# The first x tile loaded in two column halves, and the first value product moved up between two transposes

## The chip, the cores and the metric

The kernel runs on one core of one Trainium2 chip. The metric is the device time of one execution in microseconds (us), lower is better. The time before is 286.43 us, the median of three runs that lie between 286.04 and 286.88 us.

## The reference

The reference mixes two branches over the same x of 2048 tokens by 640 columns, in bfloat16, with a gate per token. Branch a is a linear attention with 32 heads of 20 columns and softmax feature maps; branch b is a SwiGLU block with 1728 hidden columns.

```python
x = A_x                                             # 1 x 2048 x 640
g = _sigmoid((x * gate_w).sum(-1, keepdims=True))
qkv = x @ wqkv                                      # q, k, v of 32 heads
...
kv = jnp.einsum("bhsf,bhsd->bhfd", phi_k, v)
...
a = o @ wo
b = (silu(x @ w_gate) * (x @ w_up)) @ w_down
return g * a + (1 - g) * b
```

## The kernel before, in words

**Tiling.** The 2048 tokens are 16 tiles of 128 tokens. For most products the kernel needs x transposed, with the 640 columns as 5 chunks of 128 on the partitions: the buffer `xT` holds chunk c of tile t as `xT[:, t, c, :]`. Tiles 0 to 3 are loaded as they are into `xs` and transposed by TensorE (PE) against an identity, with a copy from PSUM to `xT` behind it; tiles 4 to 15 are transposed by the DMA. The value weights are in `wvg`, five chunks of 128 rows with 640 columns, and one more column (640) that the kernel fills with `gate_w`, so that one product gives the values and the gate's sum.

**Order.** Nothing reorders the program. Two strings list it: `LOADS` gives the order in which the loads are issued, and `ORDER` that of the work. A small recorder (`run`, line 145) adds the waits on semaphores that the buffers' readers and writers need. Each engine goes through its own instructions in that order, so an instruction that waits holds back all that stands behind it on its engine. One call of `mm` (line 302) or `transposes` (line 319) is one unit for the recorder: all that any of its matmuls reads must be there before its first one starts.

**Queues.** Loads are issued by SP and by ACT, each through a DMA queue of its own. `XQ` and `WQ` (lines 376 and 377) give the issuer of each x tile and each value weight chunk. SP issues x tile 0, gate_w (`g`), w1, w2, w3 and then the first columns of the gate and up weights (`f0`); ACT issues w0, x1, x2, x3, w4 and, behind these, loads its activation table and does its copies.

**The work around the change.** `H0` to `H12` are 26 matmuls on a constant that feed nothing. `X0.0` transposes chunk 0 of tile 0 (its copy is on DVE), `X0.1` chunks 1 to 4 (its copy is on ACT); `X1` and `X2` do both parts of tiles 1 and 2 with both copies on DVE, `X3` does tile 3 in one part. `G` turns gate_w into a column with one small matmul, and DVE casts it into column 640 of `wvg`. `Ut.c` (`vpart`, line 525) adds chunk c of the value product of tile t: two matmuls of 320 and 321 columns, one for each half of the columns, into the two PSUM banks of a pair. Only the second half reads column 640. `U0.0` is thus the first product with real data; it needs `xT` chunk 0 of tile 0 and w0, and as one unit also the column from `G`. `h` is a step that ACT alone runs: it waits for w3 and issues two small loads. From `F0.1` on the feed-forward products follow, whose weights are `f0`.

PSUM is used as four pairs of banks; `next_pair` (line 475) gives the one that was used longest ago. `U1.0` writes the pair that `X0` used, so it also waits until both copies of `X0` have read it.

Of the kernel before, what the change touches and what calls it, by code (L numbers as in the profile page):

```python
# [6 lines left out]
P = 128  # L7
S_TOK = 2048
D = 640
# [21 lines left out]


LOADS = """
x0 w0 x1 g w1 x2 w2 x3 w3 w4 f0 k0 k1 t4 k2 k3 k4 k5 t5 t6 t7 t8 t9 t10 t11 t12 t13 t14 t15 q0 q1 q2 q3 q4 q5
 f1 f2
"""

ORDER = """
H0 H1 H2 H3 H4 H5 H6 H7 H8 H9 H10 H11 H12 X0.0 G X0.1 X1 h U0.0 U1.0 U0.1 X2 U1.1 U2.0 U0.2 U1.2 U2.1 X3 U2.2
U0.3 U1.3 U2.3 U0.4 U1.4 U2.4 V3 Y i4 F0.1 M0 M1 F0.2 M2 V4 M3 M4 F0.0 M5 K0 i3 K1 S0 I P0 K3 S1 P1  # L40
F1.0 K2 V6 E0 V8 K4 S2 S3 E1 S4 K5 S5 P2 P3 V7 E2 V5 R0 K6 P4 P5 R2 E3 K7 S6 E4 V15 K8 E5 V10 S7 P6
K9 E6 R1 P7 S8 K10 S9 E7 K11 S10 V9 V11 P8 E8 K12 P9 R3 E9 P10 K13 S11 E10 K14 S12 P11 V12 S13 E11
# [11 lines left out]
class _Tracker:  # L54
# [90 lines left out]
    def run(self, eng, fn, reads=(), writes=(), dma=False):  # L145
        rkeys = list(dict.fromkeys(k for a in reads for k in self.keys_of(a)))
        wkeys = list(dict.fromkeys(k for a in writes for k in self.keys_of(a)))
        need = {}

        def req(ev, raw):  # L150
            if ev is None:
                return
            s, v = ev
            if s == eng and not dma and (eng == "pe" or not raw):
                return
            if v > need.get(s, 0):
                need[s] = v

        for k in rkeys:
            for kk in self._conflicts(k):  # L160
                req(self.lastw[kk], True)
                if k[0] == "psum":
                    for s, v in self.readers[kk].items():
                        req((s, v), False)
        for k in wkeys:
            for kk in self._conflicts(k):
                req(self.lastw[kk], True)
                for s, v in self.readers[kk].items():
                    req((s, v), False)
        self._wait(eng, need)  # L170
        ins = fn()
        if dma:
            sn = "d%d" % self.ndma
            self.ndma += 1
            self._add_sem(sn)
            inc = 16
        else:
            sn, inc = eng, 1
        ins.then_inc(self.sem[sn], inc)
        self.cnt[sn] += inc  # L180
        v = self.cnt[sn]
        snap = dict(self.known[eng])
        if not dma:
            snap[sn] = max(snap.get(sn, 0), v)
        self.evknow.setdefault(sn, {})[v] = snap
        ev = (sn, v)
        for k in wkeys:
            self.lastw[k] = ev
            self.readers[k] = {}
        for k in rkeys:  # L190
            r = self.readers[k]
            if r.get(sn, 0) < v:
                r[sn] = v
        return ev


def _build(nc, A_x, A_wqkv, A_w_phi, A_wo, B_x, B_w_gate, B_w_up, B_w_down, gate_w, out):
    tr = _Tracker(nc)
    pe, act, dve, pool, sp = nc.tensor, nc.scalar, nc.vector, nc.gpsimd, nc.sync
# [68 lines left out]
    def at(name, shape, dtype, rel):  # L268
        n = mybir.dt.size(dtype)
        for s in shape[1:]:  # L270
            n *= s
        assert rel + n <= SLAB, (name, rel + n, SLAB)
        t = nc.alloc_sbuf_tensor_at(name, list(shape), dtype, offset=sbase + rel)
        tr.reg(t, "sbuf", sbase + rel)
        return t
# [4 lines left out]
    xs = at("xs", [P, NPE, D], BF16, 10752)  # L280
# [10 lines left out]
    def bank(b, c0, c1, r0=0, r1=P):  # L291
        return ps[r0:r1, b * 512 + c0:b * 512 + c1]
# [9 lines left out]
    def mm(pairs):  # L302
        reads, writes = [], []
        for p in pairs:
            reads += [p[1], p[2]]
            writes.append(p[0])

        def fn():
            last = None
            for o, l, r, st, sp_, sk in pairs:  # L310
                last = pe.matmul(o, lhsT=l, rhs=r, start=st, stop=sp_, skip_group_check=sk)  # L311
            return last
        return run("pe", fn, list({id(a): a for a in reads}.values()), writes)
# [45 lines left out]
    def dma(e, dst, src, transpose=False):  # L359
        eo = tr.eng[e]  # L360

        def fn():
            if transpose:
                return eo.dma_start_transpose(dst, src)
            return eo.dma_start(dst, src)  # L365
        rd = [src] if src.tensor.name in tr.base else []
        wr = [dst] if dst.tensor.name in tr.base else []
        return run(e, fn, rd, wr, dma=True)
# [7 lines left out]
    XQ = ["sp", "act", "act", "act"]  # L376
    WQ = ["act", "sp", "sp", "sp", "act"]
    x2 = A_x[0]
# [3 lines left out]
        return dma(e, dst, A_wqkv[c * P:(c + 1) * P, c0:c0 + D])  # L382

    def load_x(t):
        dma(XQ[t], xs[:, t, :], x2[t * P:(t + 1) * P, :])

    def load_xt(t):
        dma("sp", xT[:, t, :, :], x2[t * P:(t + 1) * P, :], transpose=True)
# [81 lines left out]
    def used(r):  # L470
        ring["lru"].remove(r)
        ring["lru"].append(r)
        return r

    def next_pair():
        return used([r for r in ring["lru"] if r < ring["n"] and r not in held][0])
# [31 lines left out]
    def v_pairs(t, pr):  # L508
        return [(bank(2 * pr + hb, 0, 320 + hb), xT[:, t, c, :], wvg[:, c, 320 * hb:640 + hb - 320 * (1 - hb)],
                 c == 0, c == 4, False) for c in range(5) for hb in range(2)]  # L510

    def v_out(t, pr):
        i = halves(pr).rearrange("p b (h d) -> p b h d", d=DH)
        o = vbuf(t)[:, 0:H * (DH + 1)].rearrange("p (b h d) -> p b h d", b=2, d=DH + 1)[:, :, :, 0:DH]
        copy("act", o, i)
        copy("act", svec[:, t:t + 1], bank(2 * pr + 1, 320, 321))
# [6 lines left out]
    vpr = {}  # L523

    def vpart(t, c):

        if c == 0:
            vpr[t] = next_pair()
            held.add(vpr[t])
        mm(v_pairs(t, vpr[t])[2 * c:2 * c + 2])  # L530
        if c == 4:
            held.remove(used(vpr[t]))
            v_out(t, vpr[t])
# [302 lines left out]
    def kv_end():  # L836
# [4 lines left out]

    ops = {
        "H": lambda i: warm(), "i": fills, "X": xpose, "G": gcol, "U": vpart, "V": vtile,
        "M": lambda m: premult(1, m), "R": lambda m: premult(0, m),
        "K": ktile, "S": knorm, "P": kmul, "p": lambda t: kmul(t, "dve"), "E": kvtile, "x": load_x, "t": load_xt, "w": load_wv, "g": load_gate, "h": load_phi, "k": lambda m: load_wt(1, m), "q": lambda m: load_wt(0, m),
        "f": lambda i: load_ffn(FCUT[i], FCUT[i + 1]), "L": load_late_weights, "T": tail_weights, "J": gates,
        "Y": w_blocks, "I": kv_begin, "N": kv_end, "Z": z_row,
# [50 lines left out]
```

## Time and profile before

| what | value |
|---|---|
| median of three runs | 286.43 us (286.04 to 286.88) |
| the profiled execution's own time | 286.45 us |
| its span from the first to the last instruction | 285.2 us |
| PE busy | 282.2 us, 99% of the span, 1999 matmuls |
| DVE, ACT, POOL busy | 61%, 52%, 55% |
| from 6.63 to 7.30 us: PE busy | 0.46 of 0.67 us |
| from 7.30 to 11.55 us: PE busy | 4.25 of 4.25 us |

The profile is one execution seen by the hardware profiler; times within it count from the span's start. A busy PE need not be doing useful work at its full rate: the 26 constant matmuls count as busy, and a matmul's time on the page (about 0.22 to 0.48 us in the first microseconds) is its latency, while the distance from one start to the next is what it costs when many follow each other. The chain of waits that the page prints goes back from the last instruction to what released each one; what stands on it sets the end.

### The profile page before, as it was taken

Reading aid. Unit: us, or ns where it says so; the run is one execution under the profiler, and the core shown is the slowest. Engines: PE = TensorE matmul, PEld = TensorE weight load, DVE = VectorE, ACT = ScalarE, POOL = GpSimd, SP = SyncE. Lnnn points to the kernel's source line nnn. Section 1 sums busy time; section 2 is a strip of 40 time slices with the busy share of each in tenths; the row PEclk is TensorE's granted clock in tenths of the full one; section 3 lists DMA queues with packets and bytes.
Section 4 is the critical chain, followed back from the end, with each engine's and each line's share of the span. In section 5 each row is a group of like instructions: output and inputs, shape, how many; then the busy total and the mean of one; then the engine's idle time right before and its main releaser. Section 6 shows DMA issues by size and latency. Waiting matters only on the chain.

```text
span 285.2 us, 5063 instructions
## 1 busy us (share of the span) xinstructions
PE 282.2 (99%) x1999; PEld 174.6 (61%) x1999; DVE 174.3 (61%) x265; ACT 148.1 (52%) x258; POOL 155.9 (55%) x120
## 2 busy tenths in 40 slices
PE   8999999999999999999999999999999999999997
PEld 6656777766645444545544547767767545767766
DVE  2246667784689975998799756898962627200000
ACT  2577787786755655666566676224323457321122
POOL 6186988987157759869688643473540563100000
PEclk9999999999999999999999999999999999999999
DMA  7975779100010952522031200166243030010011
GB/s 208 242 119 127 118 139 373 68 3 0 3 47 0 275 154 57 105 54 51 0 71 33 52 0 7 37 96 143 55 113 85 3 74 1 11 47 25 23 46 48
DMA packets 50727, 22.20 MB, mean 78 GB/s; under 512 B 40815, under 2 KB 50567, under 8 KB 50703
## 3 DMA queue, kind: packets, MB, share of 16 engines
q1 hardware_dynamic: 49174, 21.00, 31.7%
q10 hardware_dynamic: 1529, 0.87, 1.1%
q8 instruction: 16, 0.26, 0.4%
q14 instruction: 8, 0.07, 0.1%
HBM read 9.38 MB, written 2.62 MB: 42 GB/s over the span
## 4 chain that ended last, share of the span: by engine, by line
PE 97%; DMA 2%; SPq 0%; DVE 0%; issue 0%
PE ps L311 97%; DMA wvg<-in_A_wqkv_dram 2%; SPq L365 0%; PE ps L323 0%; DVE osb L824 0%
## 5 line engine op out<-in xcount | busy, mean ns | idle before, releaser
L311 PE MATMUL ps<-xT,wg 128*128 128x512 bf16 x260 | 64.6, 379 | 0.0
L311 PE MATMUL ps<-xT,wu 128*128 128x512 bf16 x260 | 64.6, 379 | 0.0
L339 POOL TENSOR_TENSOR hT<-hT,us 128x512 bf16<-128x512 bf16 (+1 forms) x36 | 42.1, 1175 | 33.5 <-DVE hT L343 21.6
L339 POOL TENSOR_TENSOR ph<-eq,qc 128x1320 bf16<-128x1320 bf16 x16 | 40.4, 2524 | 31.7 <-DVE qc L659 16.9
L311 PE MATMUL ps<-wqk,xT 128*128 128x320 bf16 x320 | 47.9, 299 | 0.0
L329 ACT ACTIVATE us<-ps 128x512 bf16<-128x512 f32 (+1 forms) x60 | 34.1, 568 | 20.5 <-PE ps L311 19.8
L311 PEld LDWEIGHTS ps<-xT,wu 128*128 128x128 bf16 x260 | 25.4, 98 | 30.7
L311 PEld LDWEIGHTS ps<-xT,wg 128*128 128x128 bf16 x260 | 25.1, 98 | 28.2 <-ACT oT L329 0.6
L339 POOL TENSOR_TENSOR ekr<-ekr,krec 128x1280 bf16<-128x1280 bf16 x16 | 37.3, 2358 | 5.8 <-DVE krec L353 5.8
L343 DVE SCALAR_TENSOR_TENSOR hT<-hT,ps 128x512 bf16<-128x512 bf16 (+1 forms) x39 | 24.9, 641 | 25.2 <-ACT hT L329 20.9
L311 PE MATMUL ps<-wd,hT 128*128 128x320 bf16 (+3 forms) x295 | 40.2, 296 | 0.0
L329 ACT ACTIVATE osb<-ps,omg 128x640 bf16<-128x640 f32 (+2 forms) x17 | 12.4, 755 | 52.9 <-PE ps L311 52.9
L311 PEld LDWEIGHTS ps<-wqk,xT 128*128 128x128 bf16 x320 | 30.5, 98 | 12.6
L311 PEld LDWEIGHTS ps<-wd,hT 128*128 128x128 bf16 (+1 forms) x295 | 26.9, 98 | 11.1 <-issue 1.3
L329 ACT ACTIVATE eq<-ps 128x640 bf16<-128x640 f32 x32 | 22.3, 703 | 19.1 <-PE ps L311 11.9
L339 POOL TENSOR_TENSOR hx<-hx,us 128x512 bf16<-128x512 bf16 (+1 forms) x20 | 24.1, 1213 | 11.5 <-DVE hx L343 5.9
L350 DVE TENSOR_REDUCE ksum<-ekr 128x64 f32<-128x1280 bf16 x16 | 23.4, 1464 | 11.0 <-ACT ekr L329 11.0
L329 ACT ACTIVATE hT<-ps 128x512 bf16<-128x512 f32 (+1 forms) x39 | 22.0, 563 | 13.4 <-PE ps L311 11.2
L329 ACT ACTIVATE ekr<-ps 128x640 bf16<-128x640 f32 x32 | 22.3, 703 | 6.9 <-PE ps L311 6.4
L311 PE MATMUL ps<-wvg,xT 128*128 128x320 bf16 (+1 forms) x160 | 24.6, 302 | 0.2 <-DMA wvg<-in_A_wqkv_dram 0.2
L311 PE MATMUL ps<-wog,oT 128*128 128x320 bf16 (+2 forms) x165 | 24.7, 295 | 0.0
L350 DVE TENSOR_REDUCE qz<-eq 128x64 f32<-128x1280 bf16 x16 | 23.4, 1480 | 1.7 <-ACT eq L329 1.7
(86 smaller groups left out, 283.7 us busy)
## 6 DMA issues: line engine op xcount, KB each, us to landing
out_dram<-osb SPq DMA_DIRECT2D x15, 160.0 KB, 1.8
wd<-in_B_w_down_dram SPq DMA_DIRECT2D x1, 2080.0 KB, 8.7
wg<-in_B_w_gate_dram SPq DMA_DIRECT2D x1, 1040.0 KB, 8.7
wu<-in_B_w_up_dram SPq DMA_DIRECT2D x1, 1040.0 KB, 10.8
wog<-in_A_wo_dram SPq DMA_DIRECT2D x2, 375.0 KB, 4.2
wg<-in_B_w_gate_dram SPq DMA_DIRECT2D x1, 640.0 KB, 5.2
wu<-in_B_w_up_dram SPq DMA_DIRECT2D x1, 640.0 KB, 6.4
xs<-in_A_x_dram ACTq DMA_DIRECT2D x3, 160.0 KB, 4.2
```

The costliest lines, as they stand in the source:

```text
L311: last = pe.matmul(o, lhsT=l, rhs=r, start=st, stop=sp_, skip_group_check=sk)
L329: return run("act", lambda: act.activation(o, i, func, scale=scale), rd, [o])
L339: return run(e, lambda: eo.tensor_tensor(o, a, b, op), [a, b], [o])
L343: return run("dve", lambda: dve.scalar_tensor_tensor(out=o, in0=a, scalar=s, in1=b, op0=op0, op1=op1), rd, [o])
L350: return run("dve", lambda: dve.tensor_reduce(o, i, AX.X, ALU.add), [i], [o])
```

## The change

Two things change, both in the first microseconds.

The load of x tile 0 becomes two: columns 0 to 383 (chunks 0 to 2, 96 KB) on SP's queue, and columns 384 to 639 (chunks 3 and 4, 64 KB) on ACT's queue. Both are the first issue of their queue, so ACT's five other loads, its table load and its copies each stand one issue further back.

In the order of the work, `X0.1` comes ahead of `G`, and `U0.0` comes between `G` and `X1`. `U0.0` is now two units for the recorder, one for each half of the columns, so that the first half doesn't wait for the gate's column. The instructions are otherwise the same, and none is added on PE, DVE or POOL. In `LOADS`, `g` and `x1` change places, but they are on different queues.

As the pairs of banks are given out in order of use, `U0` and `X1` exchange theirs (pairs 0 and 2), and with them all later users of these two; the order of reuse stays.

```diff
 LOADS = """
-x0 w0 x1 g w1 x2 w2 x3 w3 w4 f0 k0 k1 t4 ...
+x0 w0 g x1 w1 x2 w2 x3 w3 w4 f0 k0 k1 t4 ...
...
 ORDER = """
-H0 ... H12 X0.0 G X0.1 X1 h U0.0 U1.0 U0.1 X2 U1.1 U2.0 U0.2 U1.2 U2.1 X3 U2.2
+H0 ... H12 X0.0 X0.1 G U0.0 X1 h U1.0 U0.1 X2 U1.1 U2.0 U0.2 U1.2 U2.1 X3 U2.2
...
     def load_x(t):
-        dma(XQ[t], xs[:, t, :], x2[t * P:(t + 1) * P, :])
+        if t == 0:
+            for e, c0, c1 in (("sp", 0, 384), ("act", 384, D)):
+                dma(e, xs[:, t, c0:c1], x2[t * P:(t + 1) * P, c0:c1])
+        else:
+            dma(XQ[t], xs[:, t, :], x2[t * P:(t + 1) * P, :])
...
-        mm(v_pairs(t, vpr[t])[2 * c:2 * c + 2])
+        vp = v_pairs(t, vpr[t])[2 * c:2 * c + 2]
+        for m in ([vp[0:1], vp[1:2]] if t == c == 0 else [vp]):
+            mm(m)
```

## The prediction, made before the changed kernel ran

> **What bounds the kernel now.** I read the chain of waits first, cut to its first 12 us. Its columns are start, length, what.
>
> ```profile
> 1.66 0.36 SPq L365
> 2.02 0.04 issue
> 2.06 5.20 DMA wvg<-in_A_wqkv_dram
> 7.26 0.05 issue
> 7.30 0.99 PE ps L311 x6
> ```
>
> One transfer sets the start: the value weight chunk w2, issued by SP at 2.06 and landed at 7.26. At 7.30 PE begins U0.2, and from there the chain is PE to the end (97% on the page). So the change is worth what it moves U0.2's start, and nothing before 7.30 that PE can absorb in waiting. The order of time shows what PE did until then (start, length, then the work; in brackets the idle time before it and what ended it).
>
> ```profile
> 0.84 2.93 PE L504 MATMUL ps<-const-bfloat16-1.0 128*128 128x128 bf16 x26 [0.84 <-PEq L883]
> 1.26 1.42 ACTq L365 DMA_DIRECT2D xs<-in_A_x_dram  x3
> 3.19 1.28 ACT L329 ACT_TABLE_LOAD   x1 [3.19 <-issue]
> 3.69 0.10 PEld L323 LDWEIGHTS ps<-ident,xs 128*128 128x128 bf16 x1 [0.18 <-DMA xs<-in_A_x_dram]
> 3.95 0.10 PEld L311 LDWEIGHTS ps<-ident,gwr 128*128 128x128 bf16 x1 [0.16 <-DMA gwr<-in_gate_w_dram]
> 4.00 1.12 PE L323 MATMUL ps<-ident,xs 128*128 128x128 bf16 x9
> 4.63 0.60 ACT L329 ACTIVATE xT<-ps 128x512 bf16<-128x512 bf16 x1 [0.16 <-PE ps L323]
> 5.80 0.12 PEld L311 LDWEIGHTS ps<-wvg,xT 128*128 128x128 bf16 x2 [0.20 <-DMA wvg<-in_A_wqkv_dram]
> 6.10 0.44 PE L323 MATMUL ps<-ident,xs 128*128 128x128 bf16 x5
> 7.30 0.66 PEld L311 LDWEIGHTS ps<-wvg,xT 128*128 128x128 bf16 x6 [0.55 <-DMA wvg<-in_A_wqkv_dram]
> 8.41 3.43 PE L311 MATMUL ps<-wvg,xT 128*128 128x320 bf16 x24
> ```
>
> PE waits for x0 (0.18), for gate_w (0.16), for w1 (5.80) and for w2 (0.55 on the weight side; the last matmul before it starts at 6.78 and costs 0.136, so PE itself stood for 0.38). Two paces show. A transpose costs (1.12 - 0.31) / 8 = 0.10 us around 4 and (0.44 - 0.22) / 4 = 0.055 us at 6.1; a 320-column matmul costs 0.27 us at 4.92 (two take 0.74 with a last one of 0.475) and (3.43 - 0.30) / 23 = 0.136 from 8.41. PE's pace doubles between 5.45 and 5.8.
>
> Issue times plus the time to landing give the loads: x0 0.80 + 2.8 = 3.6, w0 0.80 + 3.0 = 3.8, x1 1.26 + 3.0 = 4.3, w1 1.66 + 4.1 = 5.8, x2 1.73 + 4.2 = 5.9, w2 2.06 + 5.2 = 7.3, x3 2.22 + 5.2 = 7.4, w3 2.53 + 5.6 = 8.1, w4 2.70 + 5.6 = 8.3, the gate weights 3.00 + 6.8 = 9.8, the up weights 3.48 + 7.7 = 11.2.
>
> **The change, step by step.**
>
> *x0.* Half the queue work lies in each queue, so both parts should land ahead of 3.6. The constant matmuls hold PE until 3.46 + 0.11 = 3.57, which is as early as X0.0 can be: 0.12 earlier than 3.69. If the halves land no earlier than 3.6, this is 0.
>
> *X0.1 ahead of G.* Four transposes at 0.107 follow at once, 3.67 to 4.10, and G at 4.10 finds gate_w landed (3.9). G's wait of 0.16 is covered by transposes.
>
> *U0.0.* Its first half needs DVE's copy of X0.0, which ended 0.56 after X0.0's start (3.69 to 4.25), so 4.13, and w0. w0 is now ACT's second issue: between 3.8 (where it was) and 4.3 (x1, second now, behind 160 KB instead of 64); I take 4.1, nearer the middle as it has 64 KB ahead. So it runs 4.15 to 4.42. The second half needs the gate's cast, which ended 0.40 after G's start (3.96 to 4.36): 4.50. It runs 4.52 to 4.79; 0.10 idle.
>
> *X1.* Queued behind U0.0 on PE, it goes from 4.38 to 4.79 and ends at 5.32. x1 lands between 4.3 and 4.8 (one more issue of 0.45 ahead), and is covered. DVE's copy of X1.0 ended 0.58 after X1's start: 5.37 now.
>
> *ACT's extra issue.* Three issues take 1.42, so one is 0.45 or so, and the table load goes from 3.19 to 3.64 and ends at 4.92 instead of 4.47. X0.1's copy, which waited 0.16 for PE, now waits for the table: 4.92 to 5.52 instead of 4.63 to 5.23. U1.0 writes X0's banks and waits for it; its load came 0.11 behind that copy (5.34), so 5.61 now. This loses 0.27 of what came before. Queued behind U1.0 on PE are U0.1 and all else. ACT has no other work until 8.17, where it waits for w3.
>
> *From U1.0 to U2.0.* At the fast pace: U1.0 5.61 to 5.9; U0.1 (w1 at 5.8 is there) to 6.17; X2 at 6.2, since x2 lands between 5.9 and 6.4 (one issue later; I take 6.1), to 6.48; U1.1 to 6.75; U2.0 0.63 after X2's first load, as before (6.00 to 6.63): 6.83 to 7.10. It ended at 6.92 before. So PE is ready for U0.2 at 7.10, and the most that this order can gain is 7.30 - 7.10 = 0.20 us. Were ACT's copy not late, U2.0 would end at about 6.9 and the most would be 0.4.
>
> *w2.* SP's queue has 64 KB less ahead of it, ACT's 64 KB more. From 5.0 to 8.2 the two moved 313 GB/s, so 64 KB are 0.21 us at the whole rate and 0.42 at half. Against that, w1 and w2 are issued no earlier, and from 4.2 to 5.2, where w1 and w2 were moving, the rate was only 213 GB/s, with x0 long done: then the gain is 0. I take 0.15, below the middle, as x0's bytes were through by 3.6 and w2 moved later. U0.2 would start at 7.15.
>
> *Queue arbitration.* The Trainium skill (DMA: Bandwidth & Descriptors, Queues, rings and completion order) says that each DMA engine goes round robin between the queues that have work. By that rule ACT's 64 KB more wouldn't hold w2 back, and w2 would gain the 0.42 of half the rate; the sum would then be PE's 0.20, not w2's 0.15. No row of before separates the two.
>
> *Behind U0.2.* 0.15 earlier, X3 needs x3 at 7.85 (7.4, at most 0.45 later: 7.85, just covered), U0.3 needs w3 at 8.4 (8.1), U0.4 w4 at 9.2 (8.3 to 8.8), the first feed-forward product the gate weights at 11.4 (9.8), the up weights at 12.4 (11.2). All are covered. Further on PE has no idle time that could take the gain back.
>
> *Sum:* 7.15 - 7.30 = -0.15 us. The profiled execution took 286.45 (span 285.2 and 1.25 around it), the median is 286.43: 286.3 either way.
>
> **The rivals.**
>
> *w2 does not move:* the change does what it says before 7 us, and PE waits longer for the same landing. For it: w2 is issued at the same time and moved in the slow stretch. Against it: less lies ahead. 286.4; up to 286.8 if ACT's extra bytes do cost it 0.42.
>
> *Everything lands early:* w1, x2 and w2 all come before PE is ready. PE then runs U1.0 at 5.61 and, without the wait for x2, ends U2.0 at about 7.03: 0.27 gained, 286.15. A gain above 0.4 has no mechanism here, as PE's own work and ACT's copy fill the time.
>
> *The pace doubles later (slower):* in before the pace doubled at about 5.6, after PE had been nearly without holes since 0.84. Now a hole of 0.29 (5.32 to 5.61) and one of 0.10 (4.42 to 4.52) lie right ahead of that place; in return the holes of 0.12 and 0.16 near 3.7 go. If the doubling comes later, U1.0, U0.1, U1.1 and U2.0 cost 8 x 0.13 more and X2 5 x 0.05 more: 1.3, of which 0.2 is hidden by the wait for w2: +1.1, 287.5; lasting through U0.2 to X3, seven more matmuls or so, up to 2.1. It decides if the transposes of X2 still follow each other at 0.107. The profile's granted clock is 1.00 in all stages, so only the spacing shows it. The Trainium skill (TensorE: Matmul & The Clock Gate, Part 1) puts this doubling at the end of a free-running window of about 3.4 us in which PE was busy. By that rule the moment varies from run to run; the doubling 4.7 us after PE's first matmul agrees, and what hole counts as idle no run here shows.
>
> *w0 holds X1 back:* U1.0 would follow w0's landing by 1.2 (U0.0 0.53, X1.0 and its copy 0.58, two releases). That matters only from w0 at 4.6 on; x1's row bounds it at 4.3. Every 0.1 beyond costs 0.1.
>
> **How the numbers follow.** The forecast (0 to 0.2 gained) gets 0.57, w2 unmoved 0.18, all early 0.10, the later doubling 0.13, w0 0.02. Runs of the same kernel spread from 286.04 to 286.88, so I call 0.3% (0.86 us) the limit of what can be told from no change. No case of gain reaches it by itself; with that scatter 0.07 of the forecast and 0.05 of the early case end beyond it: faster 0.12. Slower: 0.11 of the doubling, and 0.05 from scatter of the others, 0.16. The rest is 0.72. The forecast's own range, with the scatter of the median, is 285.9 to 286.7. The range 285.8 to 287.2 takes in the unmoved and early cases and the beginning of the slow one, and leaves out about 0.09 above and 0.06 below.
>
> **What would show it.** Right: X0.0 at about 3.57, G with no wait behind X0.1, U0.0 from about 4.15, ACT's table load at about 3.64 and U1.0 released by ACT's copy at about 5.6, U0.2 at 7.1 to 7.2, PE unbroken behind it. Wrong: U0.2 earlier than 7.0 (ACT's copy did not hold U1.0), at 7.3 or later with w2 its releaser (w2 unmoved), transposes at 0.107 in X2 (pace), or a new wait for x3 or w4 behind 7.3.

## The result: slower, 288.24 us against 286.15

The changed kernel takes 288.24 us (median of 19 runs, 286.72 to 290.12), the kernel before 286.15 (19 runs, 285.83 to 287.79). The ratio of the means is 1.0063, with a 95% interval from 1.005 to 1.0077. The forecast was 286.3, its range ended at 287.2.

The 19 times are not one cloud: nine lie from 286.72 to 287.58 (mean 287.2), ten from 288.24 to 290.12 (mean 289.0), and none between. So there are two costs to find: one of about 0.8 us in every execution (the lower group's mean against 286.35, the mean of before) and one of about 1.9 us in half of them. The profiled execution, 287.03 us with a span of 285.8, is of the lower group.

First the chain of waits of the changed kernel; these are its main lines from 1.25 to 7.24 us (start, length, what):

```profile
1.25 0.45 ACTq L365
...
1.73 4.20 DMA xs<-in_A_x_dram
...
5.97 0.24 PE ps L323
...
6.24 0.23 DVE xT L335
...
6.52 0.72 PE ps L311 x4
```

Before, w2 headed this chain: issued by SP at 2.06, landed at 7.26. Now it is an x tile issued by ACT at 1.73 and landed at 5.93: x1, for which X1 waits. Behind it come X1's first transpose, DVE's copy of it, U1.0, and PE without another release by a load.

The order of time of the same execution shows the work up to there (idle time before it in brackets):

```profile
3.57 0.74 PE L323 MATMUL ps<-ident,xs 128*128 128x128 bf16 x5
...
3.68 1.28 ACT L329 ACT_TABLE_LOAD   x1 [3.68 <-issue]
...
4.10 0.21 PE L311 MATMUL ps<-ident,gwr 128*128 128x5 bf16 x1
4.20 0.72 PE L311 MATMUL ps<-wvg,xT 128*128 128x320 bf16 x2
4.61 0.10 PEld L311 LDWEIGHTS ps<-wvg,xT 128*128 128x128 bf16 x1 [0.31 <-DVE wvg L335]
...
4.97 0.60 ACT L329 ACTIVATE xT<-ps 128x512 bf16<-128x512 bf16 x1
...
5.97 0.45 PE L323 MATMUL ps<-ident,xs 128*128 128x128 bf16 x5 [1.05 <-DMA xs<-in_A_x_dram]
...
7.36 1.53 PE L311 MATMUL ps<-wvg,xT 128*128 128x320 bf16 x10
```

X0, G and U0.0 are done earlier than before: U0.0's first half starts at 4.20, not 4.92. Then PE stands for 1.05 us, where before it went on with X1 at 4.38. What was gained at the front is handed back at X1 with interest. U0.2 is the fifth of the ten matmuls in the last line: four at 0.136 after 7.36 put it at 7.90, against 7.30 before. That is +0.60, and the end moves by as much (287.03 - 286.45 = 0.58). In this execution the pace had already doubled in the first half of U0.0, at about 4.2, before PE stood: the transposes of X1 follow each other at 0.055.

### The profile page after: what moved, and what is told of

Same layout as the page of the kernel before. It is cut to its first block, busy times and chain, and to the rows that moved or that the text cites. A ratio compares the mean times of both kernels' runs of the same rounds, so it can differ in the third digit from the quotient of the medians.

```text
span 285.8 us, 5064 instructions
## 1 busy us (share of the span) xinstructions
PE 281.8 (99%) x1999; PEld 174.6 (61%) x1999; DVE 174.6 (61%) x265; ACT 148.1 (52%) x258; POOL 155.9 (55%) x120
## 4 chain that ended last, share of the span: by engine, by line
PE 97%; DMA 1%; ACTq 0%; DVE 0%; issue 0%
PE ps L311 97%; DMA xs<-in_A_x_dram 1%; ACTq L365 0%; PE ps L323 0%; DVE osb L830 0%; DVE xT L335 0%
```

## The experiments

Each kernel was timed together with runs of the kernel before on the same chip.

### e1: the new order alone

The loads of before, with the new `ORDER` and the split of U0.0.

```diff
-X0.0 G X0.1 X1 h U0.0 U1.0 U0.1
+X0.0 X0.1 G U0.0 X1 h U1.0 U0.1
...
-        mm(v_pairs(t, vpr[t])[2 * c:2 * c + 2])
+        for m in ([vp[0:1], vp[1:2]] if t == c == 0 else [vp]):
+            mm(m)
```

> The loads of before (x0 whole on SP; ACT issues w0, x1, x2, x3, w4), with the new order of the work alone. Theory (x1 is late because it became ACT's third issue, and the hole that this leaves on PE sometimes keeps PE's pace low): x1 lands at about 4.3 as before, X1 starts by 4.9, PE has no hole over 0.4 us before 5.3, and the time is that of before: 286.0 to 286.3, no execution above 288. Rival (the order itself costs, because X1 now stands behind U0.0, which waits for w0 and the gate's column): X1 late and above 286.9 without any change of the loads.

Measured: 286.65 us (12 runs, 285.92 to 287.11) against 286.56 for before; ratio 1.0002, 0.9991 to 1.0013. The time is that of before. It lies 0.35 above the range expected, and before lies 0.26 above it on this occasion. Of the chain of its profiled execution, and then of its order of time:

```profile
0.80 3.03 DMA xs<-in_A_x_dram
...
3.88 0.71 PE ps L323 x5
```

```profile
4.48 0.87 PE L311 MATMUL ps<-wvg,xT 128*128 128x320 bf16 x2
5.14 0.65 PE L323 MATMUL ps<-ident,xs 128*128 128x128 bf16 x5
...
6.61 1.53 PE L311 MATMUL ps<-wvg,xT 128*128 128x320 bf16 x10
```

X1 follows U0.0 at 5.14 (expected by 4.9) without a wait for its load, which had landed at 4.39. The order is not at fault, and it gains nothing that the median shows. In this execution no load behind x0 set the start: x0 landed at 3.83 (3.65 in the profile of before), and from there the chain is PE's own work. U0.2, the fifth of the ten matmuls at 6.61, started at 7.16, long after w2, which landed at 6.29 here.

### e2: the split of the load alone

The loads of the changed kernel, the order of before.

```diff
     def load_x(t):
-        dma(XQ[t], xs[:, t, :], x2[t * P:(t + 1) * P, :])
+        if t == 0:
+            for e, c0, c1 in (("sp", 0, 384), ("act", 384, D)):
+                dma(e, xs[:, t, c0:c1], x2[t * P:(t + 1) * P, c0:c1])
```

> The loads of the changed kernel with the order of before (X1 ahead of U0.0). Theory: x1 is ACT's third issue and lands at about 5.9; X1 and now U0.0 too stand behind it, so PE idles some 1.8 us (4.1 to 5.9) and the median is at least that of the changed kernel, 287.2 in the lower executions and 289 or more in the others. Rival (the order costs): without the new order the time falls back to 286.2 to 286.6.

Measured: 288.74 us (5 runs, 288.48 to 288.83), ratio 1.0077 (1.0065 to 1.0089). Two lines of its order of time:

```profile
6.15 0.71 PE L323 MATMUL ps<-ident,xs 128*128 128x128 bf16 x5 [1.81 <-DMA xs<-in_A_x_dram]
...
8.26 0.74 PE L323 MATMUL ps<-ident,xs 128*128 128x128 bf16 x5
```

PE stood for 1.81 us. The five transposes of X1 take 0.71 us here and 0.45 in the changed kernel's profile; X2 at 8.26 is slow too. The lower group is missing, which the theory had not forecast: with the longer hole, all five executions are in the upper group. Five alone prove little: if each fell there as often as in the changed kernel (17 of 28, below), all five would do so in one case of twelve.

### e4: only 4 KB more ahead of x1

Is x1 late because 64 KB more lie ahead of it in ACT's queue? Here the cut is at column 624: ACT's first issue brings 16 columns.

```diff
-            for e, c0, c1 in (("sp", 0, 384), ("act", 384, D)):
+            for e, c0, c1 in (("sp", 0, 624), ("act", 624, D)):
```

> The changed kernel with the cut of x tile 0 at column 624 instead of 384: ACT's first issue then brings 16 columns (4 KB) instead of 64 KB, SP's 156 KB. Theory (what counts is that x1 is ACT's third issue): x1 still lands at 5.5 to 6.0, PE has the same hole, median 287 to 289. Rival (the 64 KB ahead of it in ACT's queue make x1 late): x1 lands by 4.6, and the time is 286.0 to 286.5.

Measured: 288.76 us (10 runs), four from 287.04 to 287.31 and six from 288.75 to 289.65; ratio 1.0067 (1.0047 to 1.0088). X1 in its profiled execution, which took 287.11 us:

```profile
6.05 0.45 PE L323 MATMUL ps<-ident,xs 128*128 128x128 bf16 x5 [1.12 <-DMA xs<-in_A_x_dram]
```

The bytes don't matter: x1 landed at 6.00 with 4 KB and w0 ahead, and at 5.93 with 64 KB and w0. The number of packets is not tested, as 16 columns still take 128 packets, one for each row.

### e6: x1 issued later, with nothing more in the queue

The kernel before, with twelve met waits on ACT ahead of its issue of x1.

```diff
     def load_x(t):
+        if t == 1:
+            for _ in range(12):
+                act.wait_ge(tr.sem["pool"], 1)
         dma(XQ[t], xs[:, t, :], x2[t * P:(t + 1) * P, :])
```

> The kernel before with twelve waits on ACT, already met, ahead of its issue of x1: x1 is issued some 0.45 us later (about 1.7 instead of 1.26), as in the changed kernel, but stays the second transfer of its queue with only w0 ahead. Theory A (the place in the queue counts: the third issue of either queue lands at 5 to 6 whatever it carries): x1 still lands by 4.8, time 286.3 to 286.9, none above 288. Theory B (the time of issue counts): x1 lands at 5.5 to 6, PE has the hole before X1, 287.0 to 289.5.

Measured: 288.66 us (6 runs: 287.29, 287.59 and four from 288.57 to 289.27), ratio 1.0074 (1.0049 to 1.0098). From its order of time, the issues on ACT and then X1:

```profile
0.80 0.42 ACTq L365 DMA_DIRECT2D wvg<-in_A_wqkv_dram  x1
...
1.71 0.82 ACTq L365 DMA_DIRECT2D xs<-in_A_x_dram  x2
...
5.53 0.45 PEld L323 LDWEIGHTS ps<-ident,xs 128*128 128x128 bf16 x5 [1.39 <-DMA xs<-in_A_x_dram]
```

x1 is ACT's second transfer, with only w0 ahead, and lands at about 5.5. Theory A, which I had held so far, falls: x1 is a second transfer here and lands late, and all six executions took 287.29 us or more. Issued at 1.26 this load landed at 4.28; 0.45 us later it lands 1.2 us later. That the time of issue is the whole cause is not shown. A load counts as landed with the last of its 16 completion events. The eighth came at 3.96 in before, at 4.53 here and at 4.98 in the changed kernel, which issued x1 at the same time but as third transfer; here 15 had come by 4.77, and one straggler makes the 5.49. The edit also issues x2, x3 and w4 0.34 us later, and x2 landed at 7.38 (5.96 in before), so not all of this time is x1's.

Where the time goes in the changed kernel can be seen in the DMA's rate. Two stages of before first, then the same of the changed kernel (after the stage: its length, POOL's busy time, granted clock, DMA's busy share, GB/s):

```profile
3.20:4.00 0.80, 0.74 (x3) 1.00 1.07 348
4.00:4.80 0.80, 0.80 (x1) 1.00 1.04 264
```

```profile
3.20:4.00 0.80, 0.74 (x3) 1.00 0.62 154
4.00:4.80 0.80, 0.80 (x1) 1.00 0.91 302
```

And the first of these stages in e6:

```profile
3.20:4.00 0.80, 0.74 (x3) 1.00 0.93 311
```

Before, x1's packets started from 3.15 to 3.80, while the DMA as a whole moved 348 GB/s (counting the packets of ACT's queue in the order of issue). In the changed kernel the loads issued by 1.3 (both parts of x0, w0, gate_w) are 320 KB instead of 480, and their packets are through by 3.2. Those of x1 start from 3.17 on, but thinly: half of them had started by 4.18, and the DMA ran at 154 GB/s from 3.2 to 4.0. The half of x0 took the early place that x1 had, and too little was ready to fill it. In e6, where x0 is whole, there is no such gap, and x1 still lands late. So two things are shown, that x1 lands late when it is issued at 1.7 and that the DMA had room meanwhile in the changed kernel; what holds x1's packets back stays open.

### e5: the hole by itself

The loads of before, e1's order, and twenty met waits on PE between U0.0 and X1.

```diff
-X0.0 X0.1 G U0.0 X1 h U1.0 U0.1
+X0.0 X0.1 G U0.0 y X1 h U1.0 U0.1
...
+    def hole(k=20):
+        for _ in range(k):
+            pe.wait_ge(tr.sem["pe"], 1)
```

> The loads of before with the new order of the work, and twenty waits that are already met between U0.0 and X1 on PE: they hold PE for about 1.06 us (0.053 each, as in the row of 24 such waits later in the kernel) at the place where the changed kernel waits for x1. No load differs from before, and x1 has landed long before. Theory (the hole by itself, whatever makes it, costs its own length less what was hidden, and in part of the executions keeps PE's pace low): two groups of times, about 286.7 to 287.2 and about 288.3 to 289. Rival (the group near 289 comes from the changed loads): one group, 286.5 to 287.3, none above 288.

Measured: 288.24 us (9 runs), four from 286.95 to 287.05 and five from 288.24 to 288.84; ratio 1.0052 (1.0029 to 1.0076). Both groups are there, with all loads as in before. The profiled execution took 288.24 us:

```profile
5.84 0.69 PE L323 MATMUL ps<-ident,xs 128*128 128x128 bf16 x5 [0.61 <-PE ps L311]
6.42 1.25 PE L311 MATMUL ps<-wvg,xT 128*128 128x320 bf16 x4
7.47 0.74 PE L323 MATMUL ps<-ident,xs 128*128 128x128 bf16 x5
8.00 1.77 PE L311 MATMUL ps<-wvg,xT 128*128 128x320 bf16 x8
```

Four 320-column matmuls take 1.25 us, not 0.72, and X2 0.74, not 0.44: PE is still at its slow pace at 8 us. The waits ran from 4.8 to 5.7, PE's own record shows 0.61 us idle, and no load was involved: x1 had landed at 4.26. So a hole alone makes both groups.

### e3: the hole filled

The changed kernel with ten constant matmuls, which feed nothing, between U0.0 and X1.

```diff
-X0.0 X0.1 G U0.0 X1 h U1.0 U0.1
+X0.0 X0.1 G U0.0 l10 X1 h U1.0 U0.1
...
+    def filler(k):
+        for _ in range(k):
+            last = pe.matmul(bank(2 * pr, 0, P), lhsT=c, rhs=c, start=True, stop=True)
```

> The changed kernel with ten more constant matmuls (128 columns, feeding nothing) between U0.0 and X1, where PE stood idle for 1.05 us. They cost 0.55 us at the fast pace and 1.07 at the slow one, so they end before x1 lands at about 5.9. Theory (the executions near 289 are those in which the hole keeps PE at its slow pace): they vanish or become few, the median is 287.0 to 287.4 and the highest below 288. Rival (the spread comes from loads that land late): the spread stays, the median near 288.2 and a third or more of the executions above 288.5.

Measured: 287.57 us (5 runs, 287.30 to 287.88), ratio 1.0039 (1.0027 to 1.0052): the upper group is gone, the lower one stays, a little above the 287.0 to 287.4 expected. From its order of time:

```profile
4.85 1.27 PE L518 MATMUL ps<-const-bfloat16-1.0 128*128 128x128 bf16 x10
6.35 0.45 PE L323 MATMUL ps<-ident,xs 128*128 128x128 bf16 x5 [0.23 <-DMA xs<-in_A_x_dram]
...
7.46 0.44 PE L323 MATMUL ps<-ident,xs 128*128 128x128 bf16 x5
```

The load is as late as ever, X1 at 6.35, but it runs at the fast pace. The pace doubled behind the ten constant matmuls, which still follow each other at 0.107, and ahead of X1. Work that feeds nothing took 0.67 us off the median of the changed kernel's first runs (288.24), and 1.03 off that of e9 below (288.60).

### e9: the changed kernel once more

No edit; a new profile.

> The changed kernel as it is, once more on this chip, with a new profile. Theory: x1 lands between 5.4 and 6.3 again and PE has the hole; the times fall in two groups, about 287 and about 288.7, and the profile shows which pace its execution had behind the hole: near 287 the transposes of X1 follow each other at 0.055, near 289 at 0.107. Rival (the spread is in the landings): in an execution above 288.2 the pace is 0.055 and a load lands more than 1 us later than in the first profile.

Measured: 288.60 us (9 runs: 287.04, 287.83 and seven from 288.30 to 288.96), ratio 1.0061 (1.0033 to 1.0089). The profiled execution is one of 288.60 us:

```profile
6.43 0.71 PE L323 MATMUL ps<-ident,xs 128*128 128x128 bf16 x5 [1.36 <-DMA xs<-in_A_x_dram]
7.03 1.25 PE L311 MATMUL ps<-wvg,xT 128*128 128x320 bf16 x4
8.07 0.74 PE L323 MATMUL ps<-ident,xs 128*128 128x128 bf16 x5
```

x1 landed at 6.38, 0.45 later than in the first profile, and the pace is the slow one through X2. So the upper group of the changed kernel is that of e2 and e5, and the landings explain 0.45 of the 1.57 us between the two profiled executions.

### e7 and e8: loads in other early places

If the places before 1.3 are what counts, other loads could have them. In e7, made from before, ACT issues gate_w behind x1, so that w1 is SP's second issue; in e8, made from the changed kernel, x1 is SP's second issue and gate_w ACT's third, X2 comes behind U1.2, and four constant matmuls stand behind X1. Of e7's edits:

```diff
-        dma("sp", gwr[0:5, :], ...
+        dma("act", gwr[0:5, :], ...
...
-X0.0 G X0.1 X1 h U0.0 U1.0 U0.1 X2 U1.1 U2.0 U0.2 U1.2 U2.1 X3 U2.2
+X0.0 X0.1 X1 h u0.0.0 u0.1.0 u1.0.0 u1.1.0 G u0.0.1 u0.1.1 u1.0.1 u1.1.1 U0.2 U1.2
+X2 U2.0 U2.1 U2.2 X3
```

and of e8's:

```diff
-    XQ = ["sp", "act", "act", "act"]
+    XQ = ["sp", "sp", "act", "act"]
...
-X0.0 X0.1 G U0.0 X1 h U1.0 U0.1 X2 U1.1 U2.0 U0.2 U1.2 U2.1 X3 U2.2
+X0.0 X0.1 u0.0.0 X1 l4 G h u1.0.0 u0.0.1 u1.0.1 U0.1 U1.1 U0.2 U1.2
+X2 U2.0 U2.1 U2.2 X3
```

> The kernel before with gate_w issued by ACT behind x1 instead of by SP ahead of w1, so that w1 is SP's second issue, w2 its third; the column's product G and the second column halves of U0.0, U0.1, U1.0 and U1.1 come behind their first halves, and X0.1's copy is on DVE. Theory (a place earlier in the queue lands that much earlier): w1 lands at about 4.4 instead of 5 to 5.8, w2 at about 5.9 instead of 6.3 to 7.3, and the time falls to 285.8 to 286.2 against 286.4 for before. Rival (PE's own work and the copies fill the time up to 7 us): the loads land earlier, the time is that of before within 0.1%.

> The changed kernel with x1 issued second by SP (at 1.26, ahead of w1) and gate_w third by ACT in its place; order X0.0 X0.1, the first half of U0.0, X1, four constant matmuls, G (its cast on ACT behind X0.1's copy), then U1.0, U0.1, U1.1, U0.2, U1.2 and only then X2, which is now ACT's fourth issue. Theory (a load issued by 1.3 lands by about 4.5, one issued at 1.7 at 5 to 6, and a PE without long holes keeps the early doubling): x1 lands by 4.6, no execution above 288, and with w2 at about 6.6 the time is 285.5 to 286.3. Rival (moving one load into the early place only moves the wait to another): the time is no better than before, 286.3 to 287.5.

Measured: e7 287.18 us (11 runs, ten of them from 287.05 to 287.63, one 288.63), ratio 1.0036 (1.0022 to 1.0049); e8 287.47 us (12 runs, 286.66 to 288.50), ratio 1.0028 (1.0011 to 1.0046). Neither beats before. e7 missed its theory and its rival, which had the time of before within 0.1%; e8 missed its theory and lies within its rival's range. A line of e7's chain, then waits from the orders of time of e7 and e8:

```profile
1.25 3.81 DMA xs<-in_A_x_dram
```

```profile
7.19 1.71 PEld L311 LDWEIGHTS ps<-wvg,xT 128*128 128x128 bf16 x8 [0.62 <-DVE wvg L335]
```

```profile
6.50 0.39 PEld L311 LDWEIGHTS ps<-wvg,xT 128*128 128x128 bf16 x4 [0.66 <-DMA wvg<-in_A_wqkv_dram]
7.46 0.39 PEld L311 LDWEIGHTS ps<-wvg,xT 128*128 128x128 bf16 x4 [0.57 <-DMA wvg<-in_A_wqkv_dram]
```

In e7's profile w2 came at 5.48 (7.26, 6.29 and 6.46 in before, e1 and e5) and w1 at 4.86 (5.76, 4.86 and 4.79). But x1, issued at 1.25 as before, landed at 5.06, 0.7 to 0.8 us later than in those three (4.28, 4.39, 4.26): with w1 in gate_w's place, 640 KB were issued by 1.3. It headed the chain, and PE waited later for the gate column's cast. That profile is of e7's one execution above 288, at the slow pace until 8.7; what the other ten lose their 0.9 us on (287.23 in the mean, 286.36 for before) has no profile.

In e8 x1, issued at 1.26 again though x0 is still split, landed at 4.21, and PE waited for w1 (6.45) and w2 (7.41) instead. Its profile is its slowest execution too, but not for the pace, which had doubled at 3.5: PE stood 0.71 us at 16.1 for a transposed weight load, which headed the chain there. In both the early place moved the wait to another load. A better order may exist; these two are not it, and no version here beats the kernel before.

## Why the prediction was wrong

**The step that failed is X1's:** "x1 lands between 4.3 and 4.8 (one more issue of 0.45 ahead), and is covered." It landed at 5.93. I added one issue's 0.45 us to the old landing, as if landings were evenly spaced. The row for it was on the page: x2, issued at 1.73, took 4.2 us to land, and x1 is now issued at 1.73. The table of issue plus landing had the gap in it (1.26 + 3.0 = 4.3, but 1.66 + 4.1 = 5.8 and 1.73 + 4.2 = 5.9). e4 shows that fewer bytes ahead would not have changed it, and e6 that being second in the queue would not have brought 4.3 back for a load issued at 1.7; e8 shows that an issue at 1.26 does. With x1 at 5.9 my own chain gives X1 at 5.97 and, at the spacing that I used (X1 to U2.0's end: 4.79 to 7.10, without the wait for ACT's copy about 2.05), U0.2 at 8.0; it was 7.90.

**The slower rival had the mechanism of the upper group and about its price.** "The pace doubles later" was priced at +1.1 to +2.1; the two groups are 1.86 apart, and its sign, transposes at 0.107 in X2, is there in e9. But its holes were of 0.29 and 0.10 us, and I gave it 0.13; the hole was 1.05 to 1.4 and lay elsewhere, because of the step above. That its price came near is partly luck, as it was summed over other matmuls. It doesn't explain the 0.8 us of the lower group, which goes with the hole itself: U0.2 came 0.60 later in the first profile, and e5's lower group, with a hole alone, lies at 287.0.

With a hole the time is in the upper group in half of the executions or more, without one almost never; between 0.6 and 1.4 us its length makes little difference (in brackets: PE's idle time ahead of X1 in the profile): e1 (none) none of 12 executions above 288, e3 (0.23) none of 5, e5 (0.61) 5 of 9, the changed kernel (1.05 and 1.36) 17 of 28, e4 (1.12) 6 of 10, e6 (1.13) 4 of 6, e2 (1.81) 5 of 5. e7 and e8, which have one each, change too much else for this row. The kernel before had 2 of 80.

**What held.** In the first profile: X0.0 at 3.57 (forecast 3.57), G with no wait, ACT's table load at 3.68 (3.64), X0.1's copy from 4.97 (4.92), U0.0's second half at 4.61 (4.52): the front went as worked out, and bought nothing. w0 landed at 3.6, better than the 4.1 taken, so the rival of w0 is out.

**What never counted.** U1.0 was to wait for ACT's late copy until about 5.6. The copy ended at 5.57, before X1 had even started, and U1.0 came at 6.52, released by DVE's copy of X1.0. So the 0.27 us for ACT's extra issue cost nothing here.

**What was mis-sized without effect.** w2 landed at 6.59, 0.67 earlier than in the profile of before, where I took 0.15. With the loads of before, though, w2 landed at 6.29 in e1 and 6.46 in e5, against 7.26 in the profile that I worked from: the same loads differ by up to 1.0, so this gain can't be put down to the split. It also means that w2, which the whole forecast took as the bound, may not be the bound in other executions of before; in e1's profile it was not.

**Arbitration.** The Trainium skill's rule (DMA: Bandwidth & Descriptors, Queues, rings and completion order) would have put w2 0.42 earlier, by the prediction's estimate. The runs can't test it, as w2's landing differs by more than that between profiles of the same loads.

**The doubling.** The Trainium skill (TensorE: Matmul & The Clock Gate, Part 1) gives the moment of the doubling as a matter of free-running windows of about 3.4 us. The runs agree that the moment varies: the fast pace came at about 4.2 us in one profile of the changed kernel and at about 9.2 in the other. By the spacing of the matmuls it came at 3.5 in e8, 4.1 in e4, 5.5 in before and e1, by 6.3 in e3, and at 8.7 to 9.5 in e2, e5, e6, e7 and e9. In the two lower-group profiles with a hole (the changed kernel's first and e4) it came ahead of the hole, and the hole of 1.05 or 1.12 us did not undo it. In e2, e5, e6 and e9 it had not come when the hole began, and it then came only near 9. So what decides seems to be which comes first; that rests on six profiles. The Trainium skill (TensorE: Matmul & The Clock Gate, HAM oscillation) names idle gaps of over 3.4 us as the harmful ones. No run here has such a gap behind the doubling; ahead of it, the late profiles show that 0.61 us (e5) to 1.81 (e2) was enough.

The profile's granted clock was 1.000 in both profiles of the changed kernel, the slow one too. It read 0.994 in five of the first ten upper executions and 1.000 in the others, so it is no safe sign of the pace.

## What to carry to other kernels

A load at the head of a queue takes the early place of the one behind it: cost a moved load by the row of the load that was issued at that time before, not by its old landing plus the delay. Take the row as a rough guide: it shifts with what else is issued early (x1 by 0.7 in e7), and one profile of the same loads can differ from the next by 1 us. In the first 10 us of this kernel an idle hole of about 1 us on PE cost some 1.5 to 1.9 us on top of itself in a part of the executions, because the pace stayed low until 8.7 to 9.5 instead of 5.5; so look at the whole list of times, not at the median or at one profile. Where the profile's clock row reads 1.00, the distance between successive matmuls tells the pace.

## What the runs showed of the hardware that I had not expected

- Time to landing jumps with the time of issue: 160 KB issued at 1.25 or 1.26 landed at 4.2 to 4.4 (as x1 in before, e1, e5 and e8; 5.06 in e7), issued at 1.71 to 1.74 at 5.5 to 6.4 (x1 in the changed kernel, e2, e3, e4, e6 and e9), with 160, 164 or 224 KB ahead of it in its queue. w1, issued at 1.66, lies between: 4.8 to 4.9 in e1 and e5, up to 6.1 elsewhere. Why loads issued at 1.7 take so long stays open.
- A hole of 0.61 us in PE's record (e5) was enough to put off the doubling of PE's pace; with ten useless matmuls in the place of the changed kernel's hole, none of five executions was above 288.
- The same loads land up to 1.0 us apart in two executions of the same order of issues (w2 at 7.26 in before, 6.29 in e1).
